# Splitting the first two F-tile pairs by token parity, warming TensorE from a zeroed tile, and waiting late for weights, with a new instruction order

## The chip, the core and the metric

The kernel runs on one core of a Trainium2 chip. A core has a matmul engine (TensorE; PE in the profile, its weight loads PEld), a vector engine (VectorE; DVE), an engine for functions (ScalarE; ACT), a general one (GpSimd; POOL) and SyncE (SP), which here issues DMAs. Each engine works through its own queue in order; they wait for one another by semaphores. The metric is the device time of one execution in microseconds (us); less is better.

## The reference

```python
def _A_ref(x, Lambda_re, Lambda_im, B_re, B_im, C_re, C_im, log_dt, Dskip):   # S5 scan
    Lam_bar = jnp.exp(dt * Lam)
    B_bar = ((Lam_bar - 1.0) / Lam)[:, None] * Bmat
    Bu = jnp.einsum("bld,pd->blp", x + 0j, B_bar)
    for t in range(L):
        h = Lam_bar[None, :] * h + Bu[:, t, :]
        hs.append(h)
    y = 2.0 * jnp.einsum("blp,dp->bld", hseq, Cmat).real + x * Dskip[None, None, :]
    return y

def _B_ref(x, w1, b1, w2, b2):                                                # MLP
    y = _layernorm(x, axis=-1)
    h = _gelu(jnp.einsum("bsd,df->bsf", y, w1) + b1)
    return jnp.einsum("bsf,fd->bsd", h, w2) + b2

xn = _layernorm(x, axis=-1)
s = _A_ref(xn, ...)
g = _silu(_B_ref(xn, ...))
return x + s * g
```

There are 2048 tokens of width D = 448, 448 complex states, and F = 1792 hidden columns in the MLP. Inputs and output are bf16.

## The kernel before

Tokens come in 8 blocks of 256; a block's even and odd tokens (parity 0 and 1) lie side by side as two rows of 128 partitions. Two blocks make a group, so there are four groups, g = 0 to 3. For each group the kernel normalizes the rows (twice, since the MLP normalizes again), transposes them, and then has two strands.

The MLP strand: `mm1` multiplies the transposed rows `xn2T` with w1, a pair of F tiles at a time (line 728), ScalarE applies GELU (line 738), `mm2` multiplies the result `gT` with w2 over 14 tiles (line 762), VectorE adds b2 (line 765), ScalarE applies SiLU (line 766). For group 0 alone, `mm1_half` does one block at a time (b = 0, 1; line 748, GELU in line 754) so that work can start when block 0 is there. It reads all four 128-row tiles of w1 (d = 0 to 3); the fourth holds w1's last 64 rows, b1 in one further row, and zeros. `fcol` takes w1's columns with a step of the chunk's tile count (4, or 2 in the last chunk). w1 comes in four chunks of columns, each by two DMAs (`w1_c` for the first 384 rows, `w1r_c` for the last 64), and w2 in four DMAs (`w2_0` to `w2_3`).

The scan strand: `bu` multiplies with the B matrices (line 654), ScalarE copies the result out (line 658), `ssm` turns it, scans it on VectorE (line 679) and turns it back (lines 707 to 711); ScalarE copies the scan's result (line 683); GpSimd works out the carry to the next group (lines 693 to 705); `ym` multiplies with the C matrices (lines 792, 795, 798), VectorE multiplies that with the gate (line 801) and adds the rest (line 804), and SyncE writes it out. In the last block the odd rows go in two parts of 256 and 192 columns, and ScalarE's queue issues the output of the second one. `skip` makes three 448-wide products or sums per block for the D skip and x; each may run on GpSimd or on VectorE (lines 776 and 777).

The start: DMAs bring x, w1 and the parameters. TensorE runs 28 matmuls of the identity with itself (line 828; the identity is made by GpSimd), then the parameter matmuls (line 480). `first_norm` handles block 0 by parity: statistics (lines 393, 394), a factor from ScalarE (lines 395, 396), scaling (line 398), four transposes on TensorE (line 401), five more identity matmuls (line 403), a copy from PSUM into `xn2T` (line 405). Block 1 is scaled in line 448, transposed in line 464 and copied in line 470. Every `mm1_half` of block 0 waits for the copies of both parities.

What sets the order: each step is a `Task` with the names that it reads and writes. `link` makes the dependencies, and `emit` walks through the list `ORDER`, puts each task on its engine's queue, and waits, ahead of a task's first instruction, for the semaphores of all it depends on, those of its own engine too. `SECOND` lists the tasks that take the second of two engines. The numbers in both lists are those of the tasks in the order of their making; names such as W0 (a copy of w1's last rows to the other half of the partitions) or H25 (the first half of `mm1` for group 2, pair 5) are tags.

## Time and profile before

| | us |
|---|---|
| median of 3 timed runs | 155.80 (155.68 to 155.81) |
| the profiled execution's own time | 155.18 |
| its span, first to last instruction | 153.1 |

| engine | busy us | share of the span | instructions |
|---|---|---|---|
| TensorE | 148.4 | 97% | 1079 |
| VectorE | 131.3 | 86% | 275 |
| ScalarE | 102.5 | 67% | 175 |
| GpSimd | 47.3 | 31% | 122 |

Rows of the profile give, for a timeline: start in us, length in us, engine, line, operation, output<-inputs, shape, count, and in brackets the idle time ahead and who ended it. Several instructions of a kind in a row are merged into one row with a count. For a line or group: count, then durations in ns (least, median, most, or busy us and mean). The chain lists the work that ended last, followed back from the end. Ends of matmuls are modelled, and they overlap: the distance between starts tells their rate.

### The profile page before, as it was taken

What the parts mean: (1) busy time and instruction counts of PE and PEld (TensorE: products, weight loads), DVE (VectorE), ACT (ScalarE), POOL (GpSimd) and SP (SyncE); (2) the same over time, 40 slices, a digit from 0 to 9 for tenths busy, and PEclk for the clock granted to TensorE, in tenths of its full rate; (3) what the DMA queues carried; (4) which work ended last, traced back from release to release, by engine and by line L of the source; (5) the groups of instructions that cost most, each with busy time, mean ns of one, the idle gap of its engine ahead of it and who ended that gap; (6) DMA issues with size and microseconds to landing.
All of it is one profiled execution on the core that took longest, in us unless ns stands there. A gap on an engine that the chain in (4) does not pass through costs nothing.

```text
span 153.1 us, 3017 instructions
## 1 busy us (share of the span) xinstructions
PE 148.4 (97%) x1079; PEld 89.9 (59%) x1079; DVE 131.3 (86%) x275; ACT 102.5 (67%) x175; POOL 47.3 (31%) x122
## 2 busy tenths in 40 slices
PE   6999999999999999999999999999999999999992
PEld 6899945454575555755544556665555665555551
DVE  5879999999988999999859998349699539999784
ACT  3876959999885688798993599841419987244110
POOL 6465896374520004700000079000512920000001
PEclk9999999999999999999999999999999999999999
DMA  4998999996859553000003310042300100010103
GB/s 115 311 259 268 349 175 238 211 187 130 160 88 175 88 103 69 0 2 0 4 1 59 84 40 0 0 96 84 62 2 0 62 0 4 0 62 0 60 0 120
DMA packets 31512, 14.04 MB, mean 92 GB/s; under 512 B 25733, under 2 KB 31113, under 8 KB 31498
## 3 DMA queue, kind: packets, MB, share of 16 engines
q1 hardware_dynamic: 31344, 13.80, 39.5%
q8 instruction: 8, 0.13, 0.4%
q10 hardware_dynamic: 154, 0.06, 0.1%
q14 instruction: 6, 0.05, 0.1%
HBM read 6.20 MB, written 1.84 MB: 53 GB/s over the span
## 4 chain that ended last, share of the span: by engine, by line
PE 85%; SPq 6%; DMA 5%; issue 1%; DVE 1%
PE psum L762 28%; PE psum L728 22%; PE psum L654 15%; PE psum L792 13%; SPq L90 6%; DMA w_sb<-in_B_w_dram 5%; PE psum L795 4%; PE psum L636 3%; PE psum L798 1%; PE psum L642 1%; DVE t L801 0%; DVE tmp L804 0%; PE psum L638 0%; PE psum L644 0%
## 5 line engine op out<-in xcount | busy, mean ns | idle before, releaser
L762 PE MATMUL psum<-w_sb,gT 128*128 128x448 bf16 x224 | 44.3, 353 | 0.1
L728 PE MATMUL psum<-xn2T,w_sb 64*128 64x512 bf16 x294 | 33.9, 378 | 0.0
L762 PEld LDWEIGHTS psum<-w_sb,gT 128*128 128x128 bf16 x224 | 21.8, 98 | 19.8 <-DMA w_sb<-in_B_w_dram 0.4
L738 ACT ACTIVATE gT<-psum,b1f 128x512 bf16<-128x512 f32 x42 | 26.0, 687 | 6.9 <-PE psum L728 6.7
L728 PEld LDWEIGHTS psum<-xn2T,w_sb 64*128 64x128 bf16 x294 | 15.6, 109 | 16.1 <-issue 3.0
L654 PE MATMUL psum<-xnT,BT 128*128 128x256 bf16 x196 | 24.1, 273 | 0.0
L654 PEld LDWEIGHTS psum<-xnT,BT 128*128 128x128 bf16 x196 | 18.4, 98 | 6.5 <-issue 3.3
L766 ACT ACTIVATE g_sb<-o 128x448 bf16<-128x448 f32 x16 | 9.1, 572 | 12.2 <-DVE o L765 12.1
L801 DVE TENSOR_TENSOR t<-psum,g_sb 128x448 bf16<-128x448 f32 (+2 forms) x17 | 10.0, 591 | 5.9 <-PE psum L795 2.8
L679 DVE TENSOR_TENSOR_SCAN s_f<-cw,cur,v_sb 128x256 f32<-128x256 f32 x21 | 14.9, 737 | 0.1
L693 POOL TENSOR_TENSOR cwk<-s_f,ang 128x3 f32<-128x3 f32 x3 | 1.4, 470 | 43.3 <-DVE s_f L679 43.3
L748 PE MATMUL psum<-xn2T,w_sb 128*128 128x256 bf16 x112 | 12.6, 273 | 0.3 <-DVE xn2T L405 0.3
L748 PEld LDWEIGHTS psum<-xn2T,w_sb 128*128 128x128 bf16 x112 | 11.9, 111 | 0.7 <-issue 0.4
L792 PE MATMUL psum<-CZ,h_sb 128*128 128x448 bf16 x56 | 11.9, 353 | 0.0
L765 DVE TENSOR_TENSOR o<-psum,b2bc 128x448 f32<-128x448 f32 x16 | 9.7, 614 | 1.7 <-PE psum L762 1.7
L792 PE MATMUL psum<-CQ,h_sb 128*128 128x448 bf16 (+2 forms) x54 | 10.5, 332 | 0.0
L683 ACT ACTIVATE s_b<-s_f 128x1536 bf16<-128x1536 f32 x4 | 5.9, 1485 | 6.7 <-DVE s_f L679 6.7
L658 ACT ACTIVATE u_sb<-psum 128x512 bf16<-128x512 f32 x12 | 7.2, 598 | 4.6 <-PE psum L654 4.6
L448 DVE TENSOR_SCALAR xn_sb<-x_all,lnw 128x448 bf16<-128x448 bf16 (+1 forms) x30 | 9.9, 364 | 0.3
L754 ACT ACTIVATE gT<-psum 128x512 bf16<-128x512 f32 x14 | 8.2, 592 | 2.7 <-PE psum L748 2.7
L804 POOL TENSOR_TENSOR tmp<-t,xr 128x192 bf16<-128x192 bf16 x1 | 0.5, 548 | 26.3 <-DVE t L801 26.3
L792 PEld LDWEIGHTS psum<-CZ,h_sb 128*128 128x128 bf16 x56 | 5.3, 98 | 5.1 <-issue 0.5
(160 smaller groups left out, 236.9 us busy)
## 6 DMA issues: line engine op xcount, KB each, us to landing
out_dram<-tmp SPq DMA_DIRECT2D x7, 224.0 KB, 1.9
x_all<-in_A_x_dram SPq DMA_DIRECT2D x3, 448.0 KB, 4.7
w_sb<-in_B_w_dram SPq DMA_DIRECT2D x3, 448.0 KB, 7.3
w_sb<-in_B_w_dram SPq DMA_DIRECT2D x3, 384.0 KB, 4.4
Bn<-in_A_B_im_dram SPq DMA_DIRECT2D x1, 336.0 KB, 8.5
Bn<-in_A_B_re_dram SPq DMA_DIRECT2D x1, 336.0 KB, 8.7
x_all<-in_A_x_dram SPq DMA_DIRECT2D x2, 112.0 KB, 2.1
x_all<-in_A_x_dram SPq DMA_DIRECT2D x1, 224.0 KB, 2.7
```

The lines of the kernel that those rows point to most:

```text
L90: return e.dma_start(out_ap, in_ap)
L448: on = [("dve", [lambda e, o=o, i=i: e.tensor_scalar(o, i, rs, nb, op0=ALU.mult, op1=ALU.add) for o, i in pairs], 0.4, 0.12), ("act", [lam ...
L654: fns = [lambda e, r=r, m=m, d=d: e.matmul(psum[:, 4, r * NK:(r + 1) * NK], BT[:, m, d, :], xnT[:, gx, d, :], start=(d == 0), stop=(d == 6 ...
L679: dve(lambda e, i=i, ri=ri, init=init: e.tensor_tensor_scan(s_f[:, i, ri, :], col(R2, i).to_broadcast([128, NK]), v_sb[:, i, ri, :], init, ...
L728: return lambda e: e.matmul(psum[:, b0 + k, :], w1_sb[halves[h], d, fcol(2 * j + k)], rhs[halves[h], d, :, :], start=first and d == 0, sto ...
L738: act([lambda e, k=k: e.activation(gT[:, gb, 2 * j + k, :], psum[:, b0 + k, :], ACT.Gelu_apprx_tanh, bias=b1f[:, 2 * j + k:2 * j + k + 1]) ...
L748: fns = [lambda e, k=k, d=d: e.matmul(psum[:, banks[k], :].rearrange("p (r c) -> p r c", r=2)[:, :, cs], w1_sb[:, d, fcol(2 * j + k)], rhs ...
L762: fns = [lambda e, fi=fi: e.matmul(psum[:, bk, 0:D], gT[:, gb, fi, q * 128:(q + 1) * 128], w2_sb[:, fi, :], start=(fi == 0), stop=(fi == N ...
L765: dve(lambda e: e.tensor_tensor(o2[:, ob, :], psum[:, bk, 0:D], b2bc[:], ALU.add), [f"ps{bk}", "b2bc"], [f"oo{ob}"], 0.62, prio - 76)
L766: act(lambda e: e.activation(g_sb[:, gs, :], o2[:, ob, :], ACT.Silu), [f"oo{ob}"] + (["silu"] if g == 0 else []), [f"g{gs}"], 0.58, prio - ...
L792: fns = [lambda e, k=k: e.matmul(psum[:, bk, c0:c1], h_sb[:, hb, k, k0:k0 + 128], cm[:, k, c0:c1], start=(k == 0), stop=False) for k in ra ...
L801: dve(lambda e: e.tensor_tensor(t3[:, fb, c0:c1], psum[:, bk, c0:c1], g_sb[:, gs, c0:c1], ALU.mult), [f"ps{bk}", f"g{gs}"], [f"t3{fb}_{c0} ...
```

## The change

- The first two pairs of F tiles of block 0 (j = 0 and 1) are no longer one task each. Two tasks take both pairs, one for each parity: 16 matmuls of 128 columns each, in place of 2 x 8 of 256. The first waits for the copy of parity 0 alone. The second does not wait for the first (`behind`), which is ahead of it on the same engine. Both GELUs wait for the second.
- A task can wait later than at its start: `late` maps an instruction's number in the task to names, whose semaphores are waited for ahead of that instruction. `mm1_half` waits for `w1r_c` ahead of its seventh matmul, and group 0's `mm2` for `w2_1`, `w2_2` and `w2_3` ahead of its 5th, 9th and 13th.
- The matmuls ahead of the first work read a tile `still`, which VectorE zeroes as its first instruction, and are 9 of 512 columns in place of 28 of 128. The five behind each parity's transposes write bank 4 in place of 3.
- In the last block, the output of the odd rows' first 256 columns is issued by ScalarE's queue and that of the other 192 by SyncE's.
- `ORDER` and `SECOND` are new. On TensorE the parameter matmuls stand behind the first parity's transposes, all of block 0's halves ahead of block 1's transposes, the last half of block 1 behind the first group of `mm2`, and in the last block the odd rows' 192-column part ahead of the even rows. On VectorE the scaling of parity 0 stands ahead of parity 1's second statistics step. Of the products of `skip`, ten move from VectorE to GpSimd and four from GpSimd to VectorE. By the order ScalarE changes between its GELU and SiLU tables 10 times in place of 12.

```diff
-    __slots__ = ("eng", "ins", "reads", "writes", "sem", "idx", "deps", "chain", "alts", "tag")
+    __slots__ = ("eng", "ins", "reads", "writes", "sem", "idx", "deps", "chain", "alts", "tag", "late", "ldeps", "behind")
...
             for k in t.reads:
                 if k in last:
                     t.deps.add(last[k])
+            for i, keys in t.late.items():
+                t.ldeps[i] = {last[k] for k in keys}
+                for k in keys:
+                    readers.setdefault(k, []).append(t)
...
-            need = {}
-            for d in t.deps:
-                sem, val = done[d]
-                if need.get(sem, 0) < val:
-                    need[sem] = val
-            for sem, val in need.items():
-                if seen.get(sem, 0) < val:
-                    eng.wait_ge(self.sems[sem], val)
-                    seen[sem] = val
             for k, fn in enumerate(t.ins):
+                need = {}
+                for d in t.ldeps.get(k, ()) if k else t.deps - {t.behind}:
+                    sem, val = done[d]
+                    if need.get(sem, 0) < val:
+                        need[sem] = val
+                for sem, val in need.items():
+                    if seen.get(sem, 0) < val:
+                        eng.wait_ge(self.sems[sem], val)
+                        seen[sem] = val
                 last = fn(eng)
...
 ORDER = ...
-10 0 18 22 1 19 23 20 16 15 88 2 21 11 3 9 27 26 12 8 17 14 13 89 24 5 7 90 25 6 4 91 28 96 29 45 97 30 92 98 93 46 31 99 94 47 48 63 103 95
-53 100 32 49 101 54 50 102 33 51 52 106 114 64 44 65 55 108 105 B0 56 116 115 B1 107 109 B2 57 117 58 B3 42 118 38 110 120 39 119 40 144 122
...
-585 594 586 595 603 597 598 601 602 611 604 607 612 605 613 606 608 614 609 610
+ST 0 18 22 10 88 1 19 23 16 20 15 2 21 11 3 9 27 26 12 8 17 14 13 24 89 5 7 25 6 90 4 91 28 96 29 92 97 30 93 98 94 45 31 99 95 46 32 100 48
+64 103 101 53 102 114 49 33 54 63 105 50 44 52 106 65 115 B0 DH 55 108 51 107 B1 109 118 116 B2 56 117 B3 120 119 42 57 122 38 110 121 58 39
...
+515 594 600 595 591 611 597 592 603 598 601 602 612 613 607 604 614 605 608 606 609 610
 SECOND = ...
-142 143 144 145 146 147 149 161 167 169 197 199 205 207 221 223 227 229 231 284 285 286 391 392 394 395 419 423 428 496 501 524 525 529 590 591 592 594 595 613 W0
+142 143 144 145 146 148 149 169 175 177 197 203 209 219 221 223 284 289 322 390 393 394 422 423 425 426 428 429 497 524 525 528 529 531 535 591 595 613 W0 W2
...
+        still = SB("still", [128, 128])
...
+            kb.tag = "ST"
+            dve(lambda e: e.memset(still[:], 0.0), [], ["still"], 0.1, S0)
...
+            LATE = ((1, 4), (2, 8), (3, 12))
...
-                    pe([lambda e: e.matmul(psum[:, 3, 0:128], ident[:, :], ident[:, :], start=True, stop=True) for _ in range(5)],
-                       [f"xm0p{par}", "ident"], ["ps3"], 0.3, 3 * PINNED + 1)
+                    pe([lambda e: e.matmul(psum[:, 4, 0:128], ident[:, :], ident[:, :], start=True, stop=True) for _ in range(5)],
+                       [f"xm0p{par}", "ident"], ["ps4"], 0.3, 3 * PINNED + 1)
...
-                fns = [lambda e, k=k, d=d: e.matmul(psum[:, banks[k], :].rearrange("p (r c) -> p r c", r=2)[:, :, cs],
-                                                    w1_sb[:, d, fcol(2 * j + k)],
-                                                    rhs[:, d, :, :], start=(d == 0), stop=(d == 3))
-                       for k in range(2) for d in range(4)]
-                ws = [chunk[2 * j]]
-                pe(fns, (["xmT0p0", "xmT0p1"] if b == 0 else ["xmT0_1"]) + [f"w1_{c}" for c in ws] + [f"w1r_{c}" for c in ws] + ["w1b"], [f"ps{k}" for k in banks], 0.89, prio)
+                wk = [f"w1_{chunk[2 * j]}", "w1b"]
+
+                def part(k, d, r, i=j):
+                    return lambda e: e.matmul(psum[:, (0, 2, 4)[(7 * b + i) % 3] + k, :].rearrange("p (r c) -> p r c", r=2)[:, r, cs],
+                                              w1_sb[:, d, fcol(2 * i + k)], rhs[:, d, r, :], start=(d == 0), stop=(d == 3))
+
+                if b == 0 and j == 0:
+                    for r in range(2):
+                        pe([part(k, d, slice(r, r + 1), i) for i in range(2) for d in range(4) for k in range(2)], [f"xmT0p{r}"] + wk, [f"ps{k}" for k in range(4)], 0.89, prio)
+                        kb.tasks[-1].late = {6: ["w1r_0"]}
+                    kb.tasks[-1].behind = kb.tasks[-2]
+                elif b or j > 1:
+                    pe([part(k, d, slice(0, 2)) for d in range(4) for k in range(2)], (["xmT0p0", "xmT0p1"] if b == 0 else ["xmT0_1"]) + wk, [f"ps{k}" for k in banks], 0.89, prio)
+                    kb.tasks[-1].late = {6: [f"w1r_{chunk[2 * j]}"]}
...
-                pe(fns, [f"gT{gb}_{fi}_{b}" for fi in range(NF)] + [f"w2_{c}" for c in range(4)], [f"ps{bk}"], 2.66, prio)
+                pe(fns, [f"gT{gb}_{fi}_{b}" for fi in range(NF)] + [f"w2_{c}" for c in range(1 if g == 0 else 4)], [f"ps{bk}"], 2.66, prio)
+                if g == 0:
+                    kb.tasks[-1].late = {w: [f"w2_{c}"] for c, w in LATE}
...
-                        kb.dma("act" if c0 else "sp", dram_ap(out, off + par * D + c0, [[2 * D, 128], [1, w]]), o_sb[:, ob, par * D + c0:par * D + c1], reads=[f"o{ob}_{par}_{c0}"],
+                        kb.dma("act" if par and not c0 else "sp", dram_ap(out, off + par * D + c0, [[2 * D, 128], [1, w]]), o_sb[:, ob, par * D + c0:par * D + c1], reads=[f"o{ob}_{par}_{c0}"],
...
-            pe([lambda e: e.matmul(psum[:, 3, 0:128], ident[:, :], ident[:, :], start=True, stop=True) for _ in range(28)],
-               ["ident"], ["ps3"], 2.8, 3 * PINNED)
+            pe([lambda e: e.matmul(psum[:, 3, :], still[:, :], still[:, None, :].to_broadcast([128, 4, 128]), start=True, stop=True) for _ in range(9)],
+               ["still"], ["ps3"], 2.8, 3 * PINNED)
```

32 lines of the change are left out of this document (17 added, 15 removed).

## The prediction

> **What bounds the kernel now.** I read the profile page first (busy time, chain), then the chain in order of time, then the first 13 us engine by engine, then the end. The page:
>
> ```profile
> PE 148.4 (97%) x1079; PEld 89.9 (59%) x1079; DVE 131.3 (86%) x275; ACT 102.5 (67%) x175; POOL 47.3 (31%) x122
> PE 85%; SPq 6%; DMA 5%; issue 1%; DVE 1%
> ```
>
> TensorE is busy for 97% of a span of 153.1 us and carries 85% of the chain that ended last. So a change pays only where TensorE idles, where its work shrinks, or behind its last matmul. The chain in order of time shows these places:
>
> ```profile
> 9.81 0.43 SPq L90
> ...
> 11.23 8.32 DMA w_sb<-in_B_w_dram
> ...
> 19.60 10.77 PE psum L762 x56
> 30.37 7.73 PE psum L728 x70
> ...
> 48.92 0.76 PE psum L654 x7
> ...
> 72.01 0.87 PE psum L654 x7
> ...
> 150.11 0.12 PE psum L798
> ...
> 150.26 0.44 DVE t L801
> ...
> 150.72 0.43 DVE tmp L804
> ```
>
> TensorE's second product (line 762) waits until 19.55 for the last of the four w2 transfers (11.23 + 8.32); from 19.60 TensorE works without a break of note to 150.23. The seven matmuls at 72.01 take 0.11 more than the same seven at 48.92: that is the one later gap I found. After 150.23 come two VectorE steps (to 151.15) and the last output.
>
> How TensorE came to its first real matmul, and how fast its small ones go (TensorE, then its weight loads):
>
> ```profile
> 5.54 0.40 PE L401 MATMUL psum<-ident,xn_sb 128*128 128x128 bf16 x4
> 5.77 0.44 PE L403 MATMUL psum<-ident 128*128 128x128 bf16 x5
> 6.50 4.53 PE L748 MATMUL psum<-xn2T,w_sb 128*128 128x256 bf16 x40 [0.28 <-DVE xn2T L405]
> 10.99 0.62 PE L464 MATMUL psum<-ident,xn_sb 128*128 128x128 bf16 x8
> 1.41 2.91 PEld L828 LDWEIGHTS psum<-ident 128*128 128x128 bf16 x28 [1.41 <-POOL mhalf L314]
> 10.98 0.45 PEld L464 LDWEIGHTS psum<-ident,xn_sb 128*128 128x128 bf16 x8 [0.23 <-DVE xn_sb L448]
> ```
>
> The last row gives 0.056 us for each load-and-matmul pair of 128 columns (0.45 less one load of 0.1, over 7), the third 0.109 for 256 columns (4.53 less 0.27, over 39), so 0.873 for a half pair of F tiles (8 matmuls). The 28 dummies went at 0.104.
>
> VectorE and ScalarE ahead of that:
>
> ```profile
> 4.30 0.18 DVE L394 BATCH_NORM_AGGREGATE lnmv<-lnst 128x2 f32<-128x6 f32 x1
> 4.41 0.40 DVE L398 TENSOR_SCALAR xn_sb<-x_all,lnmv,lnw 128x448 bf16<-128x448 bf16 x1
> 5.08 0.40 DVE L398 TENSOR_SCALAR xn_sb<-x_all,lnmv,lnw 128x448 bf16<-128x448 bf16 x1 [0.28 <-ACT lnw L396]
> 5.45 0.94 DVE L405 COPY xn2T<-psum 128x512 bf16<-128x512 bf16 x2
> 10.54 0.39 DVE L448 TENSOR_SCALAR xn_sb<-x_all,lnw 128x448 bf16<-128x448 bf16 x1
> 11.65 0.69 DVE L470 COPY xn2T<-psum 128x1024 bf16<-128x1024 bf16 x1 [0.72 <-PE psum L464]
> 4.17 0.20 ACT L396 ACTIVATE lnw<-lnw 128x1 f32<-128x1 f32 x1
> 4.52 0.29 ACT L395 ACTIVATE lnw<-lnmv,eps 128x1 f32<-128x1 f32 x1
> 4.84 0.20 ACT L396 ACTIVATE lnw<-lnw 128x1 f32<-128x1 f32 x1
> ```
>
> **Dummies.** The tile of zeros costs VectorE some 0.1 us at 1.04, where nothing waits until 2.9. TensorE then starts near 1.2 instead of 1.41. Nine matmuls of 512 columns are 36 dummies' worth: 36 x 0.104 = 3.7 us, to about 4.95. The transposes of the first parity, now ahead of the parameter matmuls, need the scaled rows (4.41 + 0.40 = 4.81), so the dummies cost them 0.1, which is covered below: the copy of their result waits for something else. The late wait for w1's last rows costs and brings nothing: line 748 waited for both w1 transfers of chunk 0 and began at 6.50, when VectorE's copy was ready, so they had landed. The first 26 transfers on SyncE's queue keep their order, and with it their landings.
>
> **The start, step by step.** The new VectorE order puts the first scaling (line 398) ahead of the second aggregate (394). The first scaling waits for ScalarE's 4.37 either way. The aggregate moves from 4.30 behind it, to 4.78 (the next operation begins 0.37 after a scaling: 5.08, 5.45), and ends at 4.96. ScalarE's pair, 0.52 long, then ends at 5.52 instead of 5.04, the second scaling runs 5.56 to 5.96, the second transposes start at 6.02, and with the five dummies behind them (0.23 + 0.28) TensorE is free at 6.53. The copy for parity 0 stands behind the second scaling: 5.93 to 6.40; the copy for parity 1 waits for the transposes: 6.46 to 6.88. Line 748 began 0.11 after a copy's end, so the pass over parity 0 starts at 6.53 and takes 16 x 0.056 = 0.90, to 7.43; parity 1 is ready by then (6.99) and ends at 8.33. Before, the same two pairs ended at 6.50 + 16 x 0.109 = 8.24. So the split itself brings nothing: 0.09 lost, since the reordered aggregate delays what the split was to start early.
>
> Four halves follow (to 11.82), then the eight transposes of block 1. Their rows were ready at 10.93 and are 0.49 later, 11.42: the 0.12 of idle ahead of them (6.50 + 5 x 0.873 = 10.87, started 10.99) is gone. They end at 12.44, the copy at 13.17, and the first half of block 1 starts at 13.27; only one half (0.87) now lies under the copy, where there were two, so TensorE idles 0.13. Six halves later, at 18.51, the second product starts with the first w2 chunk. Its second chunk is wanted 4 x 0.19 later (19.27), the third at 20.0, the fourth at 20.8, against 19.55 for the last and earlier issues from 9.81 on for the others. Each of these waits would hold all that TensorE has behind it; if the second chunk came only with the last, that would be 0.3. The remaining half lies between the first two groups. So line 728 starts at 18.51 + 0.87 + 10.77 = 30.15 instead of 30.37: **0.22 gained**.
>
> **From 30 to 150 us** the new order must keep TensorE fed. Both orders change between kinds of matmul equally often where that costs (11 runs of line 728), so the work is the same. I followed the queues of each engine with the durations of the rows and found no new wait; the gap at 72 goes, because the seven matmuls are followed by others than line 792: **0.11 gained**, 0 to 0.15. ScalarE saves two table loads, which are off the path.
>
> **The end.**
>
> ```profile
> 148.97 0.95 DVE L801 TENSOR_TENSOR t<-psum,g_sb 128x448 bf16<-128x448 f32 x2 [0.37 <-DVE tmp L804]
> 149.84 0.38 DVE L804 TENSOR_TENSOR tmp<-t,x_all 128x448 bf16<-128x448 bf16 x1
> out_dram<-tmp SPq DMA_DIRECT2D x1, 64.0 KB, 1.6
> out_dram<-tmp ACTq DMA_DIRECT2D x1, 48.0 KB, 1.6
> ```
>
> The 192-column part is now multiplied ahead of the even rows' eleven matmuls, so only seven 256-column matmuls (0.76) lie behind these. With T for TensorE's end: the even rows' product starts at T - 0.72, takes 0.62, its addition ends at T + 0.31, and the last product and addition, 0.42 and 0.43, end at T + 1.13 instead of T + 0.92. **0.21 lost.** The last output goes by ScalarE's queue instead of SyncE's, at 1.6 us either way.
>
> **Sum.** -0.22 - 0.11 + 0.21 = -0.12 us on the profiled 155.18 us. The timed median, 155.80, stands 0.6 above that execution; I carry the difference over: 155.7. About 0.2% (0.31 us) is what a measurement of this kernel can tell from no change; my sum lies within it.
>
> **A rule against the change.** GpSimd gets six more of the 448-wide products (ten come from VectorE, four go back).
>
> ```profile
> L711 DVE TENSOR_TENSOR h_sb<-pa x4: 281/290/1156, 69.4 to 142.2; 128x256 bf16<-128x256 bf16 x4
> L693 POOL TENSOR_TENSOR cwk<-s_f,ang x3: 193/193/1023, 59.3 to 114.1; 128x3 f32<-128x3 f32 x3
> L776 POOL TENSOR_TENSOR xr<-xd,g_sb x3: 1026/1031/1035, 29.4 to 120.1; 128x448 f32<-128x448 bf16 x3
> 89.81 2.61 POOL L702 TENSOR_TENSOR cwk<-cwk,ang 128x1 f32<-128x1 f32 x1
> ```
>
> The same operation takes 0.29 or 1.16 on VectorE, 0.19 or 1.02 on GpSimd. The Trainium skill, in "SBUF — State Buffer", section "Who interferes with whom", says why: a VectorE instruction with two SBUF inputs and a GpSimd one that reads SBUF exclude each other for a whole instruction. The trace agrees, with the numbers just given.
>
> **Rival 1: GpSimd's queue stalls TensorE near 88 us (slower).**
>
> ```profile
> L683 ACT ACTIVATE s_b<-s_f 128x1536 bf16<-128x1536 f32 x4 | 5.9, 1485 | 6.7 <-DVE s_f L679 6.7
> L679 DVE TENSOR_TENSOR_SCAN s_f<-cw,cur,v_sb 128x256 f32<-128x256 f32 x21 | 14.9, 737 | 0.1
> 6.07 1.28 ACT L754 ACT_TABLE_LOAD   x1
> 33.05 3.80 ACT L738 ACTIVATE gT<-psum,b1f 128x512 bf16<-128x512 f32 x6
> ```
>
> In the new order the carry of the fourth state tile (line 705, group 0) stands on GpSimd behind group 1's first carry steps and two products. From the end of group 1's first six scans GpSimd needs eight small steps (0.19 and some 0.07 between) and 2 x 1.03, 4.1 us; then comes the scan that waited, 0.74: 4.9 with the hand-overs near 5.1. ScalarE meanwhile copies (1.49), loads a table (1.28) and does two pairs of GELUs (a third of 3.80 each), 5.3, and then must take that scan's result ahead of the GELU that frees two banks for TensorE's next half (H25). Only 0.2 are spare. One product or step held up as above (0.8 to 2.4) uses them up: TensorE idles 0.6 or more, mostly about 1, and the time is 156.3 to 156.8. For it: the rows above; against: VectorE has few two-input operations just there. Chance 0.20.
>
> **Rival 2: 128-column matmuls with strided weights cost more than 0.056.** w1's columns are taken with a stride:
>
> ```profile
> L748 PEld LDWEIGHTS psum<-xn2T,w_sb x112: 98/113/118, 6.5 to 19.1; 128*128 128x128 bf16 x112
> L464 PEld LDWEIGHTS psum<-ident,xn_sb x8: 95/98/98, 11.0 to 11.3; 128*128 128x128 bf16 x8
> ```
>
> Such a load takes 113 ns instead of 98, and nothing of before shows it under 128 columns. The bounds are 0.056 and 0.109 (the load as the limit): 32 x 0.053 = 1.7 us at the far end; I take 0.056, since 15 ns more still hide under it. Half-way, 0.082, would lose 0.8: 156.5. The Trainium skill, in "TensorE: Matmul & The Clock Gate", section "Back-to-back issue gap", gives about 81 ns for each sustained load-and-matmul pair of 128 columns, which would give that 156.5; the trace has 56 ns for unstrided ones, against it. Chance 0.10.
>
> **Rival 3: the slow rate lasts.** The dummies at 0.104 and the transposes at 0.056 show TensorE doubling its rate near 5 us. If zeros, or the new start, put that off beyond the first 32 matmuls, they lose 32 x 0.048 = 1.5 us: 157.2. Against: the old dummies multiplied an identity, nearly all zeros too. Chance 0.05.
>
> **Chances and range.** The forecast's own case, no new wait, has the other 0.65; its terms (0.13 at 13.1, 0.22, 0.11, 0.21, each to be found or not) spread from -0.6 to +0.2: 155.2 to 156.0, about half of it faster by over 0.2%. So faster 0.33, same 0.31, slower 0.36. The range takes in rivals 1 and half of 2: 155.1 to 156.8.
>
> **What would show it.** Right: line 748's first matmul near 6.5 with 32 of 128 columns done by 8.35, the first line 762 matmul near 18.5 with no wait on w2, line 728 near 30.1, TensorE's end 0.3 earlier, the last addition 1.1 behind it. Wrong: a TensorE wait of over 0.3 on ScalarE or a DMA between 30 and 150, a pitch over 0.07 in the first 32 matmuls, or the pass over parity 0 starting before 6.3.

## The result and the profile after

| | before | after |
|---|---|---|
| median of the timed runs, us | 155.69 (155.16 to 155.81, 6 runs) | 156.45 (156.12 to 156.97, 6 runs) |
| the profiled execution's own time | 155.18 | 156.12 |
| its span | 153.1 | 154.4 |
| TensorE's end T / last addition behind it | 150.23 / +0.92 | 151.18 / +1.19 |

The ratio is 1.0056 (95% interval 1.0032 to 1.0079): slower by 0.76 us. Executions of one kernel lie over a range of 1 us and more (28 of the kernel before in one session: 154.98 to 156.52; a 29th, in the chip's slow state, is left out), so the intervals below are about 0.15 to 0.3% to each side, and what an edit does to one stage is read from the traces. One trace is one execution, and where it lay far from its kernel's median this is said.

In the profile after, the engines' busy time and the shares of the chain that ended last come first, then parts of that chain in order of time (start, length, engine, operation):

```profile
PE 149.4 (97%) x1076; PEld 88.3 (57%) x1076; DVE 128.1 (83%) x262; ACT 105.8 (69%) x181; POOL 48.5 (31%) x128
PE 92%; ACT 2%; DVE 2%; DMA 2%; issue 1%; SPq 0%; DVEq 0%; ACTq 0%
```

```profile
18.84 2.65 PE psum L780 x14
...
30.31 2.52 PE psum L738 x22
...
32.84 0.02 ACTq L139
...
32.89 1.28 ACT L748
...
34.19 1.26 ACT gT L748 x2
...
36.66 3.21 PE psum L738 x28
...
70.02 0.87 PE psum L664 x7
71.71 2.75 PE psum L780 x14
...
151.94 0.43 DVE tmp L824
```

Before, the chain ran through line 728 in one piece of 70 matmuls. After, it leaves TensorE after 22 matmuls of the same kind (line 738 now), goes by an instruction of ScalarE's queue from line 139 (that line is a wait), a load of a function table (ACT L748, 1.28) and two GELUs, and comes back to TensorE at 36.66. The w2 transfers are no longer in the chain.

TensorE after, at the start and in this stretch:

```profile
1.05 3.71 PE L848 MATMUL psum<-still 128*128 128x512 bf16 x9 [1.05 <-DVE still L301]
...
6.13 0.40 PE L411 MATMUL psum<-ident,xn_sb 128*128 128x128 bf16 x4
6.65 5.53 PE L761 MATMUL psum<-xn2T,w_sb 128*128 128x128 bf16 x64
12.01 0.61 PE L474 MATMUL psum<-ident,xn_sb 128*128 128x128 bf16 x8
30.24 5.06 PE L738 MATMUL psum<-xn2T,w_sb 64*128 64x512 bf16 x42
35.51 4.37 PE L738 MATMUL psum<-xn2T,w_sb 64*128 64x512 bf16 x36 [0.20 <-ACT gT L748]
```

The first real matmul starts at 6.65. From 30.24 on, 78 matmuls run up to the first one of line 664 at 39.81: 9.57 us, where 78 x 0.1104, the pitch of this kind without a wait, are 8.61. So 0.96 is lost here. All in all, from the two profiles:

| stretch | after less before, us |
|---|---|
| start of the span to the first matmul of line 738 (728) | -0.06 |
| from there to the first of line 664 (654), over the matmuls' own time | +0.96 |
| from there to T | +0.06 |
| T to the end of the last addition | +0.27 |
| sum | +1.23 |

The spans differ by 1.3. Two places carry the loss: the stretch from 30 to 40 us, and the end.

### The profile page after: what moved, and what is told of

The parts are those of the page before. It is cut to its first block, busy times and chain, and to the rows that moved or that the text cites. A ratio compares the mean times of both kernels' runs of the same rounds, so it can differ in the third digit from the quotient of the medians.

```text
span 154.4 us, 3013 instructions
## 1 busy us (share of the span) xinstructions
PE 149.4 (97%) x1076; PEld 88.3 (57%) x1076; DVE 128.1 (83%) x262; ACT 105.8 (69%) x181; POOL 48.5 (31%) x128
## 4 chain that ended last, share of the span: by engine, by line
PE 92%; ACT 2%; DVE 2%; DMA 2%; issue 1%; SPq 0%; DVEq 0%; ACTq 0%
PE psum L780 28%; PE psum L738 20%; PE psum L664 14%; PE psum L812 12%; PE psum L761 8%; PE psum L815 4%; PE psum L646 3%; DMA x_all<-in_A_x_dram 2%; ACT gT L748 1%; PE psum L818 1%; ACT L748 1%; DVE t L821 1%; DVE tmp L824 1%; PE psum L652 1%; PE psum L411 0%
## 5 line engine op out<-in xcount | busy, mean ns | idle before, releaser
L738 PE MATMUL psum<-xn2T,w_sb 64*128 64x512 bf16 x294 | 34.5, 378 | 0.4 <-ACT gT L748 0.2
L748 ACT ACTIVATE gT<-psum,b1f 128x512 bf16<-128x512 f32 x42 | 26.1, 687 | 1.8 <-PE psum L738 1.8
L796 POOL TENSOR_TENSOR xr<-xd,g_sb 128x448 f32<-128x448 bf16 x5 | 5.5, 1104 | 27.5 <-ACT g_sb L786 27.5
L761 PE MATMUL psum<-xn2T,w_sb 128*128 128x256 bf16 (+1 forms) x128 | 12.9, 260 | 0.0
L458 DVE TENSOR_SCALAR xn_sb<-x_all,lnw 128x448 bf16<-128x448 bf16 (+1 forms) x26 | 9.1, 386 | 2.4 <-POOL xd L796 1.2
L459 ACT ACTIVATE xn_sb<-x_all,lnw 128x448 bf16<-128x448 bf16 (+1 forms) x16 | 10.8, 702 | 0.1
```

What stands on the lines that cost most here:

```text
L458: on = [("dve", [lambda e, o=o, i=i: e.tensor_scalar(o, i, rs, nb, op0=ALU.mult, op1=ALU.add) for o, i in pairs], 0.4, 0.12), ("act", [lam ...
L459: ("act", [lambda e, o=o, i=i: e.activation(o, i, ACT.Identity, bias=nb, scale=rs) for o, i in pairs], 0.75, 0.2)]
L738: return lambda e: e.matmul(psum[:, b0 + k, :], w1_sb[halves[h], d, fcol(2 * j + k)], rhs[halves[h], d, :, :], start=first and d == 0, sto ...
L748: act([lambda e, k=k: e.activation(gT[:, gb, 2 * j + k, :], psum[:, b0 + k, :], ACT.Gelu_apprx_tanh, bias=b1f[:, 2 * j + k:2 * j + k + 1]) ...
L761: return lambda e: e.matmul(psum[:, (0, 2, 4)[(7 * b + i) % 3] + k, :].rearrange("p (r c) -> p r c", r=2)[:, r, cs], w1_sb[:, d, fcol(2 * ...
```

## The experiments

One table first, worked out from TensorE's records in each trace: the first matmul of a pair of F tiles; the first of line 738's kind (group 1); what is lost from there to the first of line 664's kind; and the time from that to T (for kernels that run 70 matmuls ahead of it, less the 8 that come later, 0.88). The ratio is to the kernel before, timed with it, as recorded; it is not the quotient of the two medians. Five groups (e1 to e4, e5 to e8, e9 to e12, e13 to e15, e16 to e18) were timed apart from one another, so across groups the ratios say more than the medians. In e6, e10, e11 and e15, which have the order of before, the first GELU's waits are kept as the kernel before has them.

| kernel | median us | ratio (95%) | first F | group 1 | lost | rest |
|---|---|---|---|---|---|---|
| before | 155.62 to 155.72 | 1 | 6.50 | 30.30 | 0.00 | 111.31 |
| after | 156.45 | 1.0056 (1.0032 to 1.0079) | 6.65 | 30.24 | 0.96 | 111.37 |
| e12: after again | 156.57 | 1.0039 (1.0012 to 1.0066) | 6.99 | 30.72 | 0.96 | 111.39 |
| e1 | 156.06 | 1.0017 (0.9996 to 1.0037) | 6.59 | 30.49 | -0.03 | 112.52 |
| e2 | 156.78 | 1.0049 (1.0026 to 1.0072) | 6.80 | 30.58 | 0.99 | 111.52 |
| e3 | 156.16 | 1.0015 (0.9995 to 1.0035) | 7.14 | 30.71 | -0.02 | 111.96 |
| e4 | 156.26 | 1.0017 (0.9995 to 1.0039) | 6.65 | 30.29 | 0.95 | 111.39 |
| e5 | 156.06 | 1.0020 (0.9990 to 1.0049) | 7.33 | 31.23 | -0.02 | 111.25 |
| e6 | 155.98 | 1.0018 (0.9996 to 1.0040) | 6.62 | 30.88 | 0.00 | 111.71 |
| e7 | 157.07 | 1.0090 (1.0076 to 1.0105) | 7.04 | 30.93 | 0.96 | 111.72 |
| e8 | 155.96 | 1.0008 (0.9981 to 1.0034) | 7.09 | 30.91 | 0.44 | 112.04 |
| e9 | 156.00 | 1.0001 (0.9972 to 1.0031) | 6.92 | 30.50 | 0.10 | 112.24 |
| e10 | 156.69 | 1.0057 (1.0026 to 1.0088) | 7.15 | 31.01 | 0.03 | 112.29 |
| e11 | 156.99 | 1.0060 (1.0035 to 1.0085) | 7.27 | 31.92 | 0.36 | 111.35 |
| e13 | 155.53 | 0.9999 (0.9968 to 1.0029) | 7.00 | 30.58 | -0.03 | 111.72 |
| e14 | 156.04 | 1.0012 (0.9985 to 1.0038) | 7.26 | 30.91 | 0.46 | 111.25 |
| e15 | 156.21 | 1.0033 (1.0006 to 1.0059) | 7.14 | 31.06 | 0.11 | 111.35 |
| e16 | 155.43 | 0.9995 (0.9969 to 1.0021) | 6.94 | 30.52 | -0.03 | 111.76 |
| e17 | 155.55 | 1.0004 (0.9980 to 1.0027) | 6.33 | 30.30 | 0.09 | 111.92 |
| e18 | 156.71 | 1.0070 (1.0048 to 1.0092) | 6.68 | 30.75 | 0.13 | 112.55 |

### The wait ahead of the table load: e1, e2, e12, e3

ScalarE around 31 us, after and then before:

```profile
30.96 0.74 ACT L459 ACTIVATE xn_sb<-x_all,lnw 128x448 bf16<-128x448 bf16 x1
32.89 1.28 ACT L748 ACT_TABLE_LOAD   x1 [1.19 <-PE psum L738]
34.19 2.42 ACT L748 ACTIVATE gT<-psum,b1f 128x512 bf16<-128x512 f32 x4
```

```profile
31.18 0.56 ACT L766 ACTIVATE g_sb<-o 128x448 bf16<-128x448 f32 x1
31.75 1.28 ACT L738 ACT_TABLE_LOAD   x1
```

Before, the load ran as soon as ScalarE was free, under TensorE's first matmuls, and the GELU (33.05, above) followed it. After, ScalarE is free at 31.70 and the load starts 1.19 later, when TensorE has finished the matmuls that the GELU reads. The load itself needs nothing of them. The first GELU of group 1 (task 365 before, 367 after) depends on several earlier steps; `emit` walks over `t.deps`, a set of objects, in an order that nobody wrote down. In the traces of before, after, e1 and e2 one of this task's two waits comes with the activation and the other stands as an instruction of its own ahead of the load. Which is which depends on the order of that walk: after, the wait for TensorE is the one ahead (the ACTq line in the chain). e1 swaps the waits of this one task in the changed kernel; e2 makes the opposite swap in the kernel before.

```diff
-                for sem, val in need.items():
+                for sem, val in sorted(need.items(), key=lambda w: t is plain[367] and w[0] != "pe"):
```

> One instruction pair of the changed kernel differs: the first GELU of group 1 waits for TensorE and for ScalarE's own last sine table, and these two waits change places, so that the table load ahead of the GELU stands behind the wait for ScalarE alone. Theory A (the lost time is a table load of 1.28 us that begins only after TensorE has filled the banks, at 32.89 us instead of about 31.7): the load runs under the matmuls, the first GELU starts near 33.05 instead of 34.19, TensorE's gaps at 35.51 and 36.66 (0.36 and 0.26 beyond the usual pitch) go, the gap at 32.95 (0.30) stays: 0.6 to 0.7 us faster than the changed kernel, 155.8. Rival B (ScalarE is late because steps were moved to it, the scaling at 30.96 and the product at 36.48): the GELUs behind the first stay late, less than 0.2 us faster, 156.3 or more. Rival C (VectorE, slowed by GpSimd's products, holds the banks): no change, 156.45.

e1's ScalarE and TensorE:

```profile
31.34 0.75 ACT L459 ACTIVATE xn_sb<-x_all,lnw 128x448 bf16<-128x448 bf16 x1
32.10 1.28 ACT L748 ACT_TABLE_LOAD   x1
```

```profile
30.49 8.65 PE L738 MATMUL psum<-xn2T,w_sb 64*128 64x512 bf16 x78 [0.25 <-ACT w_sb L863]
42.10 1.69 PE L664 MATMUL psum<-xnT,BT 128*128 128x256 bf16 x14 [0.35 <-ACT u_sb L668]
```

The load follows the activation ahead of it at once, and the 78 matmuls run in one piece of 8.65. The 0.96 is gone. But the median is only 0.4 to 0.5 lower than the changed kernel's (0.3 to 0.6 by the ratios, whose intervals overlap), and the rest of the program is 1.15 longer in the profile. That execution took 156.52, 0.46 above e1's median, so 1.15 is more than usual; the second row's wait at 42.10 is one of several that the stall had covered.

```diff
-            for sem, val in need.items():
+            for sem, val in sorted(need.items(), key=lambda w: t is plain[365] and w[0] == "pe"):
```

> The kernel before, with the two waits of group 1's first GELU in the other order: the table load stands behind the wait for TensorE. Nothing else of the order is changed. Theory A: the load moves from 31.75 to about 32.85, the first GELU from 33.05 to 34.15, TensorE stands still twice near 35 to 37 us, 0.6 to 0.9 us slower than before: 156.3 to 156.6. Rivals B and C: the kernel before has none of the moved steps and fewer products on GpSimd, so no change, 155.7.

e2's ScalarE, then TensorE:

```profile
33.24 1.28 ACT L738 ACT_TABLE_LOAD   x1 [0.97 <-PE psum L728]
```

```profile
30.58 4.74 PE L728 MATMUL psum<-xn2T,w_sb 64*128 64x512 bf16 x42
35.86 3.50 PE L728 MATMUL psum<-xn2T,w_sb 64*128 64x512 bf16 x28 [0.54 <-ACT gT L738]
```

The same loss, 0.99, comes into the kernel before, from one exchanged pair of waits: 156.78 against 155.70. e12 is the changed kernel once more, with the same 0.96 in its profile: it is no accident of one execution.

> The changed kernel itself once more, beside the others on one chip. Theory A: TensorE's three gaps between 32.9 and 36.8 are there again with 0.9 to 1.0 us beyond the usual pitch in sum, whatever the start; 156.3 to 156.5. If the time at which TensorE's rate doubles is what sets the start: the first F matmul stands between 6.59 and 7.35, with the transposes ahead of it at 0.107 or 0.056 us each.

e3 asked whether VectorE's addition of b2 (task 279, line 785), which frees a bank for TensorE and ended only at 32.89 in the profile after, was a second cause. TensorE's weight loads and VectorE after, then VectorE in e1:

```profile
32.95 1.87 PEld L738 LDWEIGHTS psum<-xn2T,w_sb 64*128 64x128 bf16 x20 [0.62 <-DVE o L785]
30.19 1.07 DVE L608 SCALAR_TENSOR_TENSOR Bn<-Bn,cw,tmp 128x448 bf16<-128x448 bf16 x1
...
32.28 0.61 DVE L785 TENSOR_TENSOR o<-psum,b2bc 128x448 f32<-128x448 f32 x1
```

```profile
30.12 0.67 DVE L608 SCALAR_TENSOR_TENSOR Bn<-Bn,cw,tmp 128x448 bf16<-128x448 bf16 x1
...
31.66 0.61 DVE L785 TENSOR_TENSOR o<-psum,b2bc 128x448 f32<-128x448 f32 x1
```

In the profile after, TensorE's matmuls halted three times: 0.30 beyond the pitch at 32.95, on this addition, and 0.36 and 0.26 at 35.51 and 36.66, on the GELUs.

```diff
 ORDER = ... (part, with e1's line)
-168 285 189 H10 417 143 279 79
+168 279 285 189 H10 417 143 79
```

> The first run's kernel, and besides VectorE's addition that empties the bank of the second product's third row tile stands ahead of two other steps (an aggregate and a product of 128 columns that took 1.08 us beside a product on GpSimd, 0.25 in the kernel before), so that it starts near 31.2 instead of 32.28. Theory A with C as a second, smaller part: the gap of 0.30 us at 32.95 goes as well, 0.9 to 1.0 us faster than the changed kernel, 155.5. If that gap was already covered by what comes behind it: as the first run, 155.8.

It changed nothing against e1, whose execution has no gap on the addition either. That is not the swap's doing: a VectorE step ahead of the addition took 0.67 there, for 1.07 after. e8 and e14 below have the swap and the gap, 0.44 and 0.46. In the changed kernel the gap adds nothing of its own, since the GELUs hold TensorE longer: e7's profile has 42 matmuls in one piece from 30.93, no gap on the addition, and the same 0.96 lost.

### The end: e4

```diff
 ORDER = ... (its end)
-595 591 611 597 592 603 598 601 602 612 613 607 604 614 605 608 606 609 610
+595 591 597 592 603 598 601 602 611 604 607 612 605 613 606 608 614 609 610
```

> The changed kernel with TensorE's and VectorE's last parts in the order of before (even rows' eleven matmuls, then the 192 columns, then the 256 columns; VectorE in step). Step of the prediction: the last addition ends T + 0.92 instead of T + 1.13 (measured T + 1.19): 0.2 to 0.27 us faster than the changed kernel, 156.2. Rival: VectorE or GpSimd is late there for another reason, no change.

The end of e4's chain:

```profile
151.27 0.43 DVE t L821
...
151.73 0.42 DVE tmp L824
```

The last addition ends 0.91 behind T, as before, where the profile after has 1.19: the 0.27 belong to the new order of the last parts. The median is 0.2 to 0.3 lower than the changed kernel's; the intervals overlap.

### The waits that stood behind it: e5, e8, e9, e13, e14, e16

e1's chain names what held the next stage (parts of it):

```profile
33.74 1.18 POOL xr L796
...
35.84 1.71 POOL lnw L434
...
47.38 4.54 DMA Cr<-in_A_C_re_dram
...
52.02 0.67 ACT tmp L605
```

Group 2's norm (task 418, line 434 on GpSimd) stands behind a product of `skip` (line 796), one of the ten moved there; and the transposing loads of C are issued by SyncE behind group 2's own transposes (in the profile after at 44.67, 46.24 and 47.56, before at 15.85, 33.72 and 39.56). ScalarE's first step on C (52.02) waits for the last one's landing. e5 puts one product (286) behind that norm:

```diff
 ORDER = ... (part, with e1's line)
-412 286 H12 367
+412 H12 367
...
-171 418 172
+171 418 286 172
```

> The kernel of the first run (waits swapped) and one product more moved: on GpSimd the fourth skip product of group 0 stands behind the steps of group 2's norm instead of ahead of them (it began at 33.74 us in the first run's profile and the norm's first step at 35.00, though VectorE's aggregates were there at 33.15). Theory D (what the first run gave back later is GpSimd's queue: norm late, so ScalarE's scaling late, so its copy of a bank late, so TensorE late): the norm's last step ends near 36.4 instead of 38.22, TensorE's gap at 42.10 (0.43 us) goes, and the smaller ones at 58 to 68 (about 0.15, 0.2 and 0.3) shrink: 0.4 to 0.7 us faster than the first run, 155.4 to 155.7. Rival E (VectorE, with its steps in another order and slowed beside GpSimd, is what is late): the gap at 42 shrinks, those at 58 to 68 stay: 155.8 to 156.0.

```profile
42.42 1.70 PE L666 MATMUL psum<-xnT,BT 128*128 128x256 bf16 x14
```

The same matmuls (line 666 in e5), which waited 0.35 in e1 at 42.10, wait no more. e5 alone can't put that down to the norm's place, since its group 1 began 0.74 later than e1's; but e9 and e16 below, with the norm ahead and group 1 at 30.50 and 30.52, have no wait there either. The median did not move (155.4 to 155.7 was expected). The rest is 111.25, but from a late start (first matmul at 7.33; see the last section), which would give every load more time (argued, not tried). e8 adds e4's end and the old place of the first scaling:

```diff
 ORDER = ... (e5 and e4, and)
-28 96 29 92 97 30 93
+28 96 29 97 30 92 93
```

> The kernel of the fifth run with the last parts in the order of before (0.27 us earlier end behind TensorE's last matmul by the trace of the fourth run) and the second aggregate ahead of the first scaling on VectorE again (the second parity's scaled rows about 0.25 us earlier). If all of it counts: 0.4 to 0.5 us faster than the fifth run, 155.0 to 155.2, faster than both kernels. If the start's gain is taken up by a wait further on: 155.3.

In its profile, of an execution 0.71 above the kernel's median, it lost 0.44 in the stretch from 30 to 40 again, by another way: TensorE waited at 33.76 for VectorE's addition. VectorE ahead of that, then GpSimd:

```profile
30.62 1.45 DVE L610 SCALAR_TENSOR_TENSOR Bn<-Bn,cw,tmp 128x448 bf16<-128x448 bf16 x1
...
32.09 1.08 DVE L569 TENSOR_SCALAR De<-ident,dcol 128x128 bf16<-128x128 bf16 x1
```

```profile
30.56 1.03 POOL L798 TENSOR_TENSOR xr<-xd,g_sb 128x448 f32<-128x448 bf16 x1 [5.31 <-ACT g_sb L788]
...
32.09 1.03 POOL L798 TENSOR_TENSOR xr<-xd,g_sb 128x448 f32<-128x448 bf16 x1
```

The operation that took 0.67 in e1 takes 1.45 beside a GpSimd product, and a small one (line 569; 0.25 in the kernel before, line 557) takes 1.08 beside the next, about as long as the product (1.03). e9 therefore puts 285 behind the norm as well, and ScalarE's copy W3 of w1's last rows (for which e1's row at 30.49 waited) earlier:

```diff
 ORDER = ... (e8, and)
-168 285 189
+168 189
...
-418 286 172
+418 285 286 172
...
-183 277 165 283 284 413 W3 288
+183 W3 277 165 283 284 413 288
```

> The kernel of the eighth run, with both products of group 0 that stood ahead of group 2's norm on GpSimd placed behind it (only one was), and ScalarE's copy of w1's last rows three steps earlier. In the eighth run's profile VectorE's product at 30.62 took 1.45 us and the one at 32.09 took 1.08 beside such GpSimd products (0.67 and 0.25 alone), the norm came 0.7 us later than in the fifth run, and TensorE waited again at 33.76, 42.58, 58.78, 59.89 and 68.44. Theory H (VectorE and GpSimd holding each other up near 30 to 33, by luck of alignment, is what these waits come from): both VectorE steps at 0.7 and 0.25, no TensorE wait beyond 0.1 us from 31 to 150; from the first matmul behind the second product to TensorE's end 120.0 us instead of 121.1; median 155.2 to 155.5. Rival I (too late a start decides: TensorE's slow rate lasted to about 6.5 us in that profile, first F matmul at 7.09): the waits go, but the time stays at 155.8 or more.

The loss there fell to 0.10; the waits on C, 58 to 68 us, stayed (rest 112.24). e13 then moves C's loads (191, 192, 193) up SyncE's queue, and e14 does that to e1 alone:

```diff
 ORDER = ... (e9 in e13, e1 in e14)
-190 376 236 192 374 377 237 193 528 529 H21 238 525 191 375
+190 376 236 374 377 237 528 529 H21 238 525 375
...
-142 195 310
+142 195 193 310
...
-273 196 177
+273 196 192 177
...
-319 H14 186
+319 H14 191 186
```

> The kernel of the ninth run, with three of C's four transposing loads issued earlier on SyncE's queue (one right behind group 2's rows near 17 us, one near 26, one ahead of two of B's; in the change all three stand behind group 2's transposes, which wait for VectorE's rows, and go out at 45.6, 46.95 and 48.27 us). In the ninth run TensorE's waits at 58.24, 59.35 and 67.89 (some 0.75 us together) remained, and ScalarE's first step on C began only at 51.89, behind these loads. Theory J (the loads of C are the last to come, once the waits ahead are gone): these three waits go, from the first matmul of line 664's kind to TensorE's end 111.3 to 111.5 us instead of 112.2; median 155.2 to 155.4. Rival K (VectorE is simply behind, whatever the loads): ScalarE's step earlier, but the waits at 58 to 68 stay, 155.9 to 156.0.

> The kernel of the first run (waits swapped, nothing else) with the same three loads issued earlier. Theory D with J: the wait at 42.10 (0.43 us, group 2's norm behind GpSimd's products) stays, those at 58.37, 59.48 and 68.03 go: 0.4 to 0.6 us faster than the first run, 155.5 to 155.7. Rival K: as the first run, 156.06.

In both, the waits on C at 58 to 68 are gone. In e13 a transpose of B now stood behind a C load and cost 0.28 at 42; e14 lost 0.46 between 30 and 40, with the GpSimd products still beside VectorE (a step of 1.28 and the small one of 1.08, and TensorE's wait at 33.77). e16 sets the loads elsewhere (191 and 193 behind 195, 192 behind 196) and has e3's place for 279.

```diff
 ORDER = ... (e9, and)
-168 189 H10 417 143 279 79
+168 279 189 H10 417 143 79
...
-190 376 236 192 374 377 237 193 528 529 H21 238 525 191 375
+190 376 236 374 377 237 528 529 H21 238 525 375
...
-142 195 310
+142 195 193 191 310
...
-273 196 177
+273 196 192 177
```

> The ninth run's kernel with the three loads of C placed so that they stand ahead of none of B's (two behind group 2's rows near 17 us, one near 26), and VectorE's addition for the third row tile ahead of the aggregate and the 128-column product beside GpSimd. In the thirteenth run B's transposes came 0.3 us late behind a load of C (TensorE's wait at 42.05). Theory A with D, H and J (all waits of TensorE between 31 and 150 us are named): none beyond 0.1 us is left, from line 664's first matmul to TensorE's end 111.3 us; 155.1 to 155.4, and faster than before by 0.2 to 0.4. Otherwise another queue takes over: 155.5 or more.

One wait of TensorE over 0.3 is left between 30 us and the end, on a transpose:

```profile
46.88 0.63 PE L740 MATMUL psum<-xn2T,w_sb 64*128 64x512 bf16 x4 [0.43 <-DMA xn2T<-xn_sb]
```

Its median is 155.43 beside 155.62 of the kernel before, ratio 0.9995 (0.9969 to 1.0021): no difference that this can tell. With the waits met that I found, this one apart, the change brings the kernel back to where it was; that it comes below is not shown.

### GpSimd's products: e10, e18

e10 gives the kernel before the new division of the 448-wide products, without the rest; e18 gives e1 the old division.

```diff
 SECOND = ... (in before)
-285 286 391 392 395 496 501 590 592 594
+289 390 393 497
```

> The kernel before with only the division of the 448-wide products changed: ten of VectorE's go to GpSimd, four of GpSimd's to VectorE, as in the change, at their old places in the order. Theory D and H: one product more stands on GpSimd ahead of group 2's norm, its last step ends near 36 instead of 35.02, VectorE's two-input steps beside GpSimd's take up to twice as long, TensorE waits 0.2 to 0.6 us between 40 and 75: 155.9 to 156.3. Rival: VectorE is relieved of six products of 0.62 us, no wait anywhere: 155.7.

VectorE, GpSimd and TensorE's weight loads in e10:

```profile
81.97 1.22 DVE L805 TENSOR_TENSOR tmp<-t,x_all 128x448 bf16<-128x448 bf16 x1
83.12 1.52 DVE L680 TENSOR_TENSOR_SCAN s_f<-cw,cur,v_sb 128x256 f32<-128x256 f32 x1
```

```profile
81.80 1.15 POOL L777 TENSOR_TENSOR xr<-xd,g_sb 128x448 f32<-128x448 bf16 x1 [16.06 <-DVE tmp L805]
83.03 1.07 POOL L777 TENSOR_TENSOR xd<-xn_sb,dbc 128x448 bf16<-128x448 bf16 x1
```

```profile
85.21 0.87 PEld L793 LDWEIGHTS psum<-CQ,h_sb 128*128 128x128 bf16 x6 [1.17 <-DVE t L802]
```

The addition takes 1.22 (0.38 alone, in the prediction's rows) and the scan 1.52 (0.74), each beside a product, and TensorE waits: from the last matmul ahead to 85.21 it is 1.07, where the same place in the kernel before has 0.31, so 0.76 is lost. Ratio 1.0057. In the order of before, the new division costs some 0.9 in all.

```diff
 SECOND = ... (in after, with e1's line)
+285 286 391 392 395 496 501 590 592 594
-289 390 393 497
```

> The kernel of the first run (waits swapped) with the 448-wide products divided between VectorE and GpSimd as before (ten back to VectorE, four to GpSimd), everything else as changed. Theory D and H: the norm of group 2 no longer stands behind a product on GpSimd and VectorE's two-input steps near 30 to 33 take 0.67 and 0.25, so TensorE's wait at 42.10 goes; 0.3 to 0.6 us faster than the first run, 155.5 to 155.7. If VectorE, with six products of 0.62 us more, is then late itself: as the first run, 156.06, or more.

The old division in the new order is worse than e1: 156.71, ratio 1.0070 (1.0048 to 1.0092), and TensorE waits at 33, 42, 58 to 60 and 68 us (0.1 to 0.6 each), with VectorE itself late; 0.5 at 8.96, on w1 (see e17), comes on top in this profile. So the order and the division belong together; neither is good in the other's place.

### The start: e7, e6, e11, e15, e17

e7 takes the split out: both pairs of F tiles in 2 x 8 matmuls of 256 columns, behind the copies of both parities.

```diff
-                    for r in range(2):
-                        pe([part(k, d, slice(r, r + 1), i) for i in range(2) for d in range(4) for k in range(2)], [f"xmT0p{r}"] + wk, ...
+                    for i in range(2):
+                        pe([part(k, d, slice(0, 2), i) for d in range(4) for k in range(2)], ["xmT0p0", "xmT0p1"] + wk, ...
```

> The changed kernel with the first two pairs multiplied pair by pair over both parities, as before, instead of parity by parity; all else as changed, the two waits too. Step of the prediction: the split brings nothing, since VectorE's new order delays what it was to start early (it reckoned 0.09 us lost): by that, the transposes of block 1 start at 12.0 as in the changed kernel, within 0.1, and the time is the same, 156.45. Rival G (the split hides the second parity's copy): the first F matmul starts at 7.1 instead of 6.65, the transposes of block 1 at 12.35, 0.3 us slower: 156.75.

TensorE in e7:

```profile
7.04 5.43 PE L761 MATMUL psum<-xn2T,w_sb 128*128 128x256 bf16 x48 [0.24 <-DVE xn2T L415]
12.31 0.61 PE L474 MATMUL psum<-ident,xn_sb 128*128 128x128 bf16 x8
```

Without the split, the first matmul comes 0.39 later than in the profile after (7.04 against 6.65) and block 1's transposes 0.30 later (12.31 against 12.01), with TensorE at its full rate before the first transposes in both profiles (see the last section): 157.07. In the changed start the split is worth about 0.3. It makes good what the start had lost: the first matmul of 256 columns came at 6.50 before and would come at 7.04 now, behind the longer dummies and the later aggregate.

e6 has all edits of the code with the order and the products of before (the tile's zeroing first, the second parity's task where the second pair's was):

```diff
 ORDER = ... (before's, and)
+ST 10 0 18
...
-106 114 64
+106 114 115 64
...
-56 116 115 B1
+56 116 B1
```

> All edits but the order: the split of the first two pairs, the zeroed tile for the dummies, the late waits, the output queues, with the order of before on every engine (and its division between VectorE and GpSimd, and its placing of the two waits). Theory A with D (the whole loss is in the order): no wait near 35 or 42, first F matmul near 6.3, second product 0.2 us earlier, the end as before: 155.3 to 155.5, 0.2 to 0.4 faster than before. Rival F (the edits themselves cost, by the split or by the waits for w2): 155.9 or more.

None of the waits at 32 to 42 us is there, so they come from the new order (and the walk over the set), not from the edits. It is still no faster than before, 155.98: with the parameter matmuls ahead of the first transposes these start at 5.50 (5.01 before), and block 1's come 5.05 behind the first matmul (6.62 to 11.67), where the kernel before has 4.49 and e2, also with before's order, 4.62.

e11 and e15 give the kernel before the late waits, with one half of block 1 moved behind the first group of `mm2` so that this can start early: in e11 the half 136, in e15 the half 140. The old dummies and the unsplit pairs stay; the exchanged output queues, the bank of the five identity matmuls and the zeroed tile, which nothing reads here, came along.

```diff
 ORDER = ... (before's; e11)
-158 136 147 160 161 275 137
+158 275 136 147 160 161 137
...
 ORDER = ... (before's; e15)
-146 140
+146 136 275 140
```

> The kernel before with the waits of the change only (line 762's groups wait for each chunk of w2 where they read it; w1's last rows late) and the first group of the second product one half pair ahead; old dummies, no split, old order elsewhere. Step of the prediction: the second product starts near 18.7 without a wait, line 728 0.2 us earlier than before (30.1), 155.4 to 155.5. Rival: a chunk of w2 lands later than it is wanted, or the banks are not free: no change, 155.7.

> The eleventh run mended: there TensorE waited 0.74 us at 23.87 because the half pair put behind the second product's first group uses the bank that its next group writes; now the half pair is put there whose banks are free, as in the change. Step of the prediction: the second product starts 0.9 us earlier than before and never waits for w2, its group behind the half pair neither, line 728 starts 0.2 us earlier than before for the same start: 155.4 to 155.5. Rival: the time moved is taken up by a wait of line 728 for the last copy of w1's rows on ScalarE: 155.7.

e11 moved the wrong half: the next group of `mm2` needs its banks, and TensorE waited 0.85 at 23.87. e15 mends that and gains nothing (1.0033, 1.0006 to 1.0059, is even above 1; what makes it slower is not shown): from block 1's transposes to `mm2`, with the half that now follows, it needs 7.59 + 0.87 = 8.46. The kernel before needs 8.61 in the profile of the prediction (10.99 to 19.60) but 8.32 and 8.33 in e2 and e10, whose first matmul came at 6.80 and 7.15: started later, it never waits for w2.

e17 cuts the five identity matmuls behind each parity's transposes to one, in e16:

```diff
-... for _ in range(5)],
+... for _ in range(1)],
```

> The kernel of the sixteenth run with one instead of five matmuls of the identity behind each of the two parities' transposes; these stand on TensorE ahead of the first F matmul and took 0.28 us per five at the high rate and 0.53 at the low one. If the start is the rest of the loss: the first F matmul 0.3 to 0.6 us earlier for the same time of doubling, 0.3 to 0.5 us faster than the sixteenth run, 154.8 to 155.0. If the second parity's copy or the low rate then holds TensorE: no change.

The first matmul came at 6.33, the earliest of all, and TensorE then waited 0.40:

```profile
8.57 0.82 PE L763 MATMUL psum<-xn2T,w_sb 128*128 128x256 bf16 x6 [0.29 <-DMA w_sb<-in_B_w_dram]
```

This is the first matmul of the third pair of F tiles, and it waits for w1's second chunk, issued at 3.28 and landed 5.15 later, at 8.43. In e18 that chunk landed at 8.82 and TensorE waited to 8.96. Over the 20 profiles it landed between 7.6 and 8.8, and the 32 matmuls ahead of this one take 1.79, so a first matmul ahead of some 6.0 to 7.2, by the execution, meets this wait. 155.55: no gain.

## Why the prediction was wrong

I predicted 155.7, no change or a little faster, from -0.22 (start), -0.11 (the gap at 72) and +0.21 (end). It came out 0.76 slower.

**"I followed the queues of each engine ... and found no new wait."** This is the step that failed. I followed when each step's inputs were ready, and not what stands in a queue ahead of its first instruction: the table load of 1.28 runs under TensorE's work or behind it, depending on which of the next activation's waits is put ahead of it. That costs 0.96 in the stretch from 30 to 40; e1 takes it out and e2 puts 0.99 into the kernel before. The sentence "a TensorE wait of over 0.3 on ScalarE or a DMA between 30 and 150" named the sign of it (0.36 at 35.51). I had written that ScalarE saves two table loads off the path; the one that stayed came onto it. Behind it were four more waits that I had not found: W3's copy, VectorE's addition beside GpSimd's products, group 2's norm behind products, and C's loads behind transposes.

**The start: 0.22 expected, 0.06 there.** `mm2` does start without a wait on w2 (18.68, forecast 18.51), and the pass of 32 matmuls has the pitch 0.056 that I took, against rival 2's 0.082. The first matmul came 0.12 later than worked out (6.65 for 6.53), since the second scaling ran at 5.68 for 5.56, and the delay goes through to line 738. More important, the yardstick was one early execution of the kernel before: the wait for w2 that the change removes (0.28) is not there when the kernel starts later, and e15 shows no gain from removing it. That the split "brings nothing" held only against the old start; against the new one it is worth 0.3 (e7).

**The gap at 72: 0.11 expected, 0 there.** The seven matmuls at 70.02 still take 0.87, and the fourteen at 71.71 take 2.75, where those at 18.84 take 2.65. Nothing was gained there.

**The end: +0.21 expected, +0.27 measured.** The mechanism was right, and e4 takes it back. T + 1.19 instead of T + 1.13.

**Rival 1** (GpSimd's queue, near 88 us) did not decide: no wait over 0.3 stands there in the profile after. That 156.45 lies in the stated range, which reaches above 156.0 only for rivals 1 and 2, is luck: neither of them made the loss. What slows single operations in rival 1 is real: e10 shows it at 85 us for 0.76, and e8 at 31 us. The Trainium skill, in "SBUF — State Buffer", section "Who interferes with whom", says that a VectorE instruction with two SBUF inputs and a GpSimd one that reads SBUF block each other whole; the rows of e8 and e10 agree (1.45 for 0.67; 1.22 and 1.52 for 0.38 and 0.74). **Rival 3** (the slow rate lasts) did not happen as put: in no profile with the split do the first 32 matmuls run at the slow rate. In some executions it lasts into the transposes ahead of them and shifts the first matmul; see the last section.

**What stays open.** The sum of e1's and e4's gains does not show whole in the medians, since other waits take over. Whether the start costs the changed kernel something in the mean over executions could not be told from one trace for each kernel.

## What to carry to other kernels

Where a function table is loaded, look at what stands ahead of the load in ScalarE's queue: put the wait for the late input with the activation and the others ahead, on purpose, not by the order of a set. A removed stall is worth what the next wait leaves of it, here some 0.3 to 0.6 of 0.96, so list the next three queues before counting the gain. A gain worked out against one early execution (the wait for w2) has to be held against a late one too.

## What the runs showed of the hardware that was not expected

The moment at which TensorE doubles its rate differs from one execution to the next far more than the start does. Two kernels with the same instructions up to here, e4 first, then e5, TensorE:

```profile
1.04 3.50 PE L848 MATMUL psum<-still 128*128 128x512 bf16 x9 [1.04 <-DVE still L301]
...
6.65 2.60 PE L761 MATMUL psum<-xn2T,w_sb 128*128 128x128 bf16 x38
```

```profile
1.04 4.02 PE L850 MATMUL psum<-still 128*128 128x512 bf16 x9 [1.04 <-DVE still L303]
...
6.64 0.57 PE L413 MATMUL psum<-ident,xn_sb 128*128 128x128 bf16 x4
...
7.33 1.84 PE L763 MATMUL psum<-xn2T,w_sb 128*128 128x128 bf16 x30
```

In e4 the nine dummies took 3.50, the rate doubling near 3.9; in e5 4.02, all at the slow rate, and the second transposes still took 0.57 for 0.40. The first real matmul came 0.68 later. Over the 20 profiles of the study the doubling lies between 3.9 us (e4) and about 7.1 (e5, e15). The profiler's mean granted clock is 1.00 both for 0 to 3.5 us of e4, where 512 columns take 0.427, and for 7 to 10 us, so it doesn't show this step; the pitch does. The Trainium skill, in "TensorE: Matmul & The Clock Gate", section "What's actually happening", has full rate after a window of about 3.4 us of activity that runs free of the kernel's start, so that the moment differs from run to run, by 500 ns to either side. The traces agree that it differs, but by far more: some 3 us lie between the earliest and the latest. The earliest, 2.9 us behind the first matmul, is also shorter than such a window.
